# Second MLP layer of eight chunks as seven block products: attention and MLP on one Trainium2 core

## The chip, the cores and the metric

The kernel runs on one core of one Trainium2 chip. The metric is the device time of one execution in microseconds. A profiled execution gives a span, from the first to the last instruction; the runs without a profile give the time that counts.

## The reference

Four sequences of 768 tokens, 8 heads of 64. Attention looks at 4 sink tokens and a window of 128; then a layer norm with gain, a two-layer MLP (512 to 2048 to 512) and the residual:

```python
scores = scale * q @ k.T ; keep = (pos < 4) | (0 <= rel < 128)
a = softmax(where(keep, scores, -1e9)) ; x = concat_heads(a @ v)        # 3072 x 512
xn = (x - mean(x)) / sqrt(var(x) + 1e-6) * g_ln
out = x + max(xn @ w_ch1, 0.0) @ w_ch2
```

## The kernel before

The 3072 tokens are 24 tiles of 128; two tiles are a *chunk*, so there are 12 chunks, c = 0 to 11. Matmuls are in bf16 with fp32 sums in PSUM.

A small planner (`Plan`) is part of the kernel: each operation is given the engines that it may run on, a cost on each, a priority (a due time made from the numbers in `PAR`) and the buffers that it reads and writes. `P.run()` lists them by a model of the engines, picks the engine and buffer, and so fixes every engine's order when the program is built. On the chip each engine goes through its own list and waits for semaphores. Tiles that change hands are taken from rings; the ring `one` has four PSUM banks, `pair` has two slots of two banks.

What a chunk goes through:

- Loads. k, q and v of a chunk are loaded by POOL's queue (`nat`, L712; `vn`, L654). From chunk 4 on, SP turns k and q by DMA transposes into `kT` and `qT` (L586). The loads of a later chunk wait for the `rs` operation of an earlier tile (`gate`).
- Attention, from tile 6 on, in `block(t)`: PE does the value products of tile t - 1 (L962, L969 for the sinks, L978), then the scores of tile t (L989) and, for an even tile, the sink scores of the chunk (L997, into a bank of ring `one`). ACT takes the exponential (L1007, L1017), DVE multiplies with the band mask (L1012). For tile t - 1 DVE takes the reciprocal (L1030) and x (L1032).
- `normalise`: DVE takes the statistics of x (L890, L892) and subtracts the mean, giving `xc` (L894). POOL makes rstd = (var + 1e-6)^-0.5 in two instructions, `rs` (L899, L900). SP transposes xc into `xnt`.
- `mlp(c)`, first layer: eight pieces `ph`, u = 0 to 7, each 8 matmuls with 256 columns (both tiles of the chunk, L1055); ACT or DVE takes the relu into a bf16 tile of 512 (`h1`, L1065, L1067). xnt is not scaled by rstd: the relu and both layers pass a positive factor through.
- `mlp(c)`, second layer: for each tile 16 matmuls with 512 columns add up in one bank (L1083). DVE multiplies with rstd and adds x in one instruction (L1092); SP stores the tile (L1096).

On PE chunk c's second layer stands around the blocks of tiles 2c + 4 and 2c + 5: 24 matmuls between the two, 8 behind the second.

Of the kernel before, what the change touches and what calls it, by code (L numbers as in the profile page):

```python
# [7 lines left out]
FP32 = mybir.dt.float32  # L8
# [202 lines left out]
def fix(occ, extra=0.09):  # L211
# [22 lines left out]
PAR = dict(strict=400.0, win=0.4, tr=-8.0, sc=-5.0, sc1=-2.0, av=2.0, blk=-8.0, step=6.0, trx=9.0, by_dma=4, x_by_dma=2,  # L234
           w1p=(1.6, 2.6, 2.7, 2.8), pm=3, w2p=(4.5, 4.51, 4.52, 4.53), apart=2, vs0=(2.0, 13.0), by_tile=0, vp=(0.0, 0.1, 2.0, 2.1, 4.55, 4.56), ld1=0.05, t0=0.8, warm=7.9, pm0=-40.0, w1g=17.0, gtt=1.25)


def general(tc, nc, slots, pairs, ones, ident_f, ident, w1, w2, mhalf, g_s, g_r, q, k, v, out, scale):
# [14 lines left out]
    xs, os_, xn, xnt, h1 = slots["ot"][0:2], slots["ot"][2:4], slots["xc"][0], slots["xnt"][0], slots["h1"]  # L253
# [117 lines left out]
def kernel(  # L371
# [12 lines left out]
    nc = tc.nc  # L384
# [42 lines left out]
    ring("h1", 34, [128, 512], BF16)  # L427
# [138 lines left out]

    recs = []
# [9 lines left out]
    rs_op, trx_op = {}, {}  # L577

# [9 lines left out]
    def by_pairs(c, what, d):  # L588
# [13 lines left out]
        def tr(e):  # L602
            for nat, pt in zip(nats, pts):
                for hp in range(HP):
# [12 lines left out]
                 writes=[x for pt in pts for x in pt], mode="h" if whole else "q")  # L617
        for (nm, src, T, ld), pt in zip(what, pts):
# [43 lines left out]
    def chunk(c):  # L662
# [3 lines left out]
        if c < 2:  # L666
            kT_b[c], qT_b[c] = Buf(f"kT{c}", "kT"), Buf(f"qT{c}", "qT")
            if c == 0:
                nats = [Buf("kf", "natf"), Buf("qf", "natf")]
                for hh in range(2):  # L670
                    hs = slice(4 * hh, 4 * hh + 4)
                    for i, (x, T) in enumerate(((k, kT_b[c]), (q, qT_b[c]))):
# [6 lines left out]
                        P.op(f"cast{nm}{hh}", {"DVE": dve(512), "ACT": act(512)}, d + 0.01 * hh,  # L679
                             lambda e, nat=nat, src=src, hs=hs: (nc.scalar.copy if e == "ACT" else V.tensor_copy)(  # L680
                                 nat.t, src.t[:, hs].rearrange("p h i d -> p i h d")),
                             reads=[part], hold=[src], writes=[nat])
# [204 lines left out]
    def normalise(c, i, d, st, x, xc):  # L887
# [6 lines left out]
        P.op(f"xc{t}", {"DVE": fix(0.26)}, d + 0.14, lambda e: V.tensor_scalar(  # L894
            xc.t, x.t, st.t[:, 14:15], None, op0=ALU.subtract), reads=[x, st, mv], writes=[xc])
        rs = Buf(f"rs{t}")
        xst_b[t, "rs"] = rs
        rs_op[t] = P.op(f"rs{t}", {"POOL": (0.83, 0.88)}, d + 5, lambda e: (
            G.tensor_scalar(st.t[:, 17:18], st.t[:, 15:16], 1e-6, None, op0=ALU.add),  # L899
            G.tensor_tensor(st.t[:, 16:17], st.t[:, 17:18], mhalf, op=ALU.pow)),  # L900
            reads=[st, mv, Bc["mhalf"]], writes=[rs])
        pt = Buf(f"ptx{t}", "one")
# [21 lines left out]
    def block(t):  # L924
        c, i, b, r = t // 2, t % 2, t // RB, t % RB
        d = at(c, "blk") + PAR["step"] * i
        last = held.get(t - 1)
        reads, writes, hold = [], [], []
        if t < NT:
# [8 lines left out]
            pp_s = Buf(f"pss{c}", "one") if sinks else None  # L938
# [3 lines left out]
            writes += pps + ([pp_s] if sinks else [])  # L942
# [15 lines left out]
        def go(e):  # L958
# [33 lines left out]
            if sinks:  # L992
                for hp in range(HP):
                    for qh in range(2):
                        u = hp // 2
                        p0 = 64 * (qh ^ u) + 32 * (hp % 2)
                        nc.tensor.matmul(pp_s.t[p0:p0 + 32, 128 * u + 64 * (not r):128 * u + 128], lhsT=kts_b[b].t[:, hp, :],  # L997
# [5 lines left out]
        if t < NT:  # L1003
# [11 lines left out]
            if sinks:  # L1015
                lo = 0 if r else 64
                P.op(f"sx{c}", {"ACT": act(256 - 2 * lo)}, d + 0.3, lambda e: nc.scalar.activation(  # L1017
                    held["ps", c].t.rearrange("p (u c) -> p u c", u=2)[:, :, lo:128],
                    pp_s.t[:, 0:256].rearrange("p (u c) -> p u c", u=2)[:, :, lo:128], AF.Exp, scale=scale),
                     reads=[pp_s], writes=[held["ps", c]])  # L1020
# [16 lines left out]
    def mlp(c):  # L1037
        T = 16.0 * c + 8.0
        xnt = xnt_b[c]
        h1 = []  # L1040
        by_tile = c < PAR["by_tile"]
        for u in range(NH1 // 2):
            ph, hb = Buf(f"ph{c}_{u}", "one"), Buf(f"h{c}_{u}", "h1")

            def mm_t(e, u=u, ph=ph):
                for s in range(4):
                    for j in range(NDM):
                        nc.tensor.matmul(ph.t[:, 128 * s:128 * s + 128], lhsT=w1[u // 2][:, j, 128 * s:128 * s + 128],
                                         rhs=xnt.t[:, j, 128 * (u % 2):128 * (u % 2) + 128], start=j == 0, stop=j == NDM - 1)
# [9 lines left out]
            o = P.op(f"ph{c}_{u}", pe(0.944 if by_tile else 0.872), pr, mm_t if by_tile else mm, reads=[xnt_t[2 * c + u % 2] if by_tile else xnt, Bw1g[u // 2] if c >= PAR["x_by_dma"] else Bw1[u // 2][u % len(Bw1[u // 2])]],  # L1059
# [3 lines left out]
            def rl(e, ph=ph, hb=hb):  # L1063
                if e == "ACT":
                    nc.scalar.activation(hb.t, ph.t, AF.Relu)  # L1065
                else:
                    V.tensor_scalar_max(hb.t, ph.t, 0.0)  # L1067
            P.op(f"rl{c}_{u}", {"ACT": act(512), "DVE": dve(512)}, pr - 3, rl, reads=[ph], writes=[hb])
            h1.append(hb)
        T += 8  # L1070
# [144 lines left out]
```

## Time and profile before

| | us |
|---|---|
| runs: median of 3 (lowest to highest) | 215.67 (214.85 to 216.92) |
| profiled execution: its span | 213.8 |
| PE busy | 207.7 (97%) |
| DVE busy | 113.9 (53%) |
| ACT busy | 110.9 (52%) |
| POOL busy | 113.7 (53%) |

The profiled execution's own time is its span plus what lies around it; no time without the profiler is given for it, and the median of the runs is 1.87 us above its span. PE is TensorE's matmuls, PEld its weight loads, DVE VectorE, ACT ScalarE, POOL GpSimd, SP the queue of stores and transposes. L1083 is line 1083 of the kernel before. Lines of the profile have the form: line, engine, operation, written tile <- read tiles, shape, count | busy us in all, mean ns of one | idle time ahead of them and what ended it.

### The profile page before, as it was taken

The page shows a single profiled execution, that of the slowest core. Times are in us where ns is not written, and L with a number is a line of the kernel's source. Part 1 is how long each engine was busy: PE and PEld are TensorE (multiplying, and loading weights), DVE is VectorE, ACT ScalarE, POOL GpSimd, SP SyncE. Part 2 cuts the span into 40 slices and gives each one's busy share as a digit, 9 for nine tenths or more (in the row PEclk, how much of TensorE's full clock was granted, in tenths as well). Part 3 has the DMA queues.
Part 4 walks back from the last instruction along what each step waited for, and adds up shares of the span by engine and source line. Part 5 has one row for each costly group of instructions (what it writes and reads, how often), then busy time and mean ns, then how long its engine had stood idle before and what let it go on. Part 6 is the DMA issues. An engine that isn't in the chain of part 4 may idle for free.

```text
span 213.8 us, 6555 instructions
## 1 busy us (share of the span) xinstructions
PE 207.7 (97%) x2699; PEld 143.0 (67%) x2699; DVE 113.9 (53%) x316; ACT 110.9 (52%) x182; POOL 113.7 (53%) x169
## 2 busy tenths in 40 slices
PE   7799999999999999999999999999999999999994
PEld 2458965755865865865865865864865865865853
DVE  5598876896365356356355456356355345444021
ACT  3798797285652652562662562562562562530610
POOL 7969842489727980980970980971970401202000
PEclk9999999999999999999999999999999999999999
DMA  5999999999999998999899899899899902202103
GB/s 153 190 188 199 190 208 194 171 178 148 142 216 144 140 129 125 117 142 187 110 148 140 112 148 127 126 143 152 109 143 143 95 3 74 77 0 74 52 0 107
DMA packets 105642, 28.04 MB, mean 131 GB/s; under 512 B 94852, under 2 KB 102664, under 8 KB 105608
## 3 DMA queue, kind: packets, MB, share of 16 engines
q0 software_dynamic: 70960, 13.18, 83.6%
q1 hardware_dynamic: 33448, 13.71, 34.8%
q10 hardware_dynamic: 1200, 0.69, 1.1%
q8 instruction: 22, 0.36, 0.7%
q14 instruction: 12, 0.10, 0.2%
HBM read 27.43 MB, written 6.29 MB: 158 GB/s over the span
## 4 chain that ended last, share of the span: by engine, by line
PE 89%; DMA 5%; DVE 3%; ACT 1%; issue 1%; ACTq 0%; DVEq 0%
PE one L1083 40%; PE one L1055 37%; DMA qT<-nat 3%; PE pair L989 3%; DMA natf<-in_q_dram 3%; PE one L962 2%; PE one L969 2%; PE one L978 1%; PE one L997 1%; DVE st L890 1%; DVE x L882 1%; PE pair L614 1%; PE pair L739 1%; PE one L867 0%; PE pair L867 0%
## 5 line engine op out<-in xcount | busy, mean ns | idle before, releaser
L1083 PE MATMUL one<-w,h 128*128 128x512 bf16 (+2 forms) x400 | 87.4, 371 | 0.0
L1055 PE MATMUL one<-xnt,w 128*128 128x256 bf16 x768 | 86.8, 273 | 0.2 <-issue 0.2
L1055 PEld LDWEIGHTS <-w 128*128 128x128 bf16 x768 | 74.7, 98 | 11.5 <-issue 0.4
L1065 ACT ACTIVATE h<-one 128x512 bf16<-128x512 f32 x94 | 56.2, 598 | 45.7 <-PE one L1055 45.7
L1083 PEld LDWEIGHTS <-h 128*128 128x128 bf16 x400 | 37.1, 98 | 40.1 <-DMA w<-in_moe_w_ch_dram 0.2
L1007 ACT ACTIVATE pe<-pair 128x768 bf16<-128x768 f32 x36 | 27.2, 808 | 41.9 <-PE pair L989 41.9
L654 POOL DMA_DIRECT2D vn<-in_v_dram x59 | 38.8, 702 | 8.5 <-DMA w<-in_moe_w_ch_dram 6.8
L899 POOL TENSOR_SCALAR st<-st 128x1 f32<-128x1 f32 x24 | 9.0, 375 | 63.8 <-DVE st L892 63.3
L1030 DVE RECIPROCAL rec<-one 128x4 f32<-128x4 f32 x36 | 6.4, 178 | 62.7 <-PE one L978 51.3
L1092 DVE SCALAR_TENSOR_TENSOR ot<-one,st,x 128x512 f32<-128x512 f32 (+2 forms) x25 | 18.2, 728 | 20.0 <-PE one L1083 13.7
L900 POOL TENSOR_TENSOR st<-st,mhalf 128x1 f32<-128x1 f32 x24 | 16.4, 682 | 2.0
L890 DVE BATCH_NORM_STATS2 st<-x 128x6 f32<-128x512 bf16 x24 | 16.7, 695 | 0.8
L1032 DVE TENSOR_TENSOR x<-one,rec 128x256 bf16<-128x256 f32 x36 | 15.3, 425 | 1.2
L712 POOL DMA_DIRECT2D nat<-in_k_dram x16 | 14.9, 935 | 1.8 <-DMA natp<-in_q_dram 1.4
L712 POOL DMA_DIRECT2D nat<-in_q_dram x16 | 14.4, 914 | 0.0
L1012 DVE TENSOR_TENSOR pe<-pe,band 128x768 bf16<-128x768 bf16 x24 | 12.2, 552 | 0.0
L894 DVE TENSOR_SCALAR xc<-x,st 128x512 bf16<-128x512 bf16 x24 | 8.9, 373 | 0.9
L989 PE MATMUL pair<-qT,kT 64*64 64x128 bf16 (+1 forms) x528 | 9.2, 204 | 0.0
L962 PEld LDWEIGHTS <-pe 128*128 128x128 bf16 (+1 forms) x144 | 6.2, 97 | 2.9 <-issue 1.3
L787 ACT ACTIVATE pe<-pair 128x1024 bf16<-128x1024 f32 (+1 forms) x8 | 7.1, 916 | 0.8 <-PE pair L739 0.4
L989 PEld LDWEIGHTS <-kT 64*64 64x64 bf16 x528 | 7.2, 108 | 0.4 <-ACT w L1119 0.4
L962 PE MATMUL one<-vn,pe 128*128 128x65 bf16 (+1 forms) x144 | 7.0, 193 | 0.0
(112 smaller groups left out, 152.3 us busy)
## 6 DMA issues: line engine op xcount, KB each, us to landing
out_dram<-ot SPq DMA_DIRECT2D x23, 256.0 KB
w<-in_moe_w_ch_dram POOLq DMA_DIRECT2D x6, 512.0 KB, 13.5
nat<-in_k_dram POOLq DMA_DIRECT2D x16, 128.0 KB, 5.0
nat<-in_q_dram POOLq DMA_DIRECT2D x16, 128.0 KB, 5.3
vn<-in_v_dram POOLq DMA_DIRECT2D x44, 32.0 KB, 5.3
w<-in_moe_w_ch_dram POOLq DMA_DIRECT2D x4, 256.0 KB, 10.9
vn<-in_v_dram POOLq DMA_DIRECT2D x15, 64.0 KB, 5.1
natp<-in_k_dram POOLq DMA_DIRECT2D x3, 256.0 KB, 6.7
```

Of the source, the lines that this page charges most:

```text
L654: P.op(f"vld{t}_{i}", {"POOL": (0.8, 0.85)}, prio + 0.001 * i, lambda e, p0=p0, n=n, hs=hs, src=src: G.dma_start(m.t[p0:p0 + n, hs, 0:64], ...
L712: lambda e, nat=nat, ap=ap: G.dma_start(nat.t, ap), writes=[nat], dma=SW, after=gate(c))
L890: P.op(f"bn{t}", {"DVE": fix(0.60)}, d + 0.12, lambda e: V.bn_stats(st.t[:, 8:14], x.t), reads=[x], writes=[st, mv])
L900: G.tensor_tensor(st.t[:, 16:17], st.t[:, 17:18], mhalf, op=ALU.pow)),
L962: nc.tensor.matmul(po[h // 4].t[:, 65 * (h % 4):65 * (h % 4) + 65], lhsT=pe_[rs, col:col + 128], rhs=vn_b[t - 1].t[rs, h, :], start=h % 4 ...
L989: nc.tensor.matmul(pps[u].t[64 * g:64 * g + 64, h2, col + c0:col + c0 + n], lhsT=kt.t[rs, hp, k0:k0 + 64], rhs=qT.t[rs, hp, q0:q0 + n], st ...
L1007: nc.scalar.activation(pes[j].t.rearrange("p a b -> p (a b)")[:, 0:768].rearrange("p (a b) -> p a b", a=2), pps[j].t[:, :, 0:384], AF.Exp, ...
L1032: P.op(f"x{t - 1}{u}", {"DVE": dve(256)}, d + 0.051 + 0.002 * u, lambda e, u=u, rc=rc, pv=pv: V.tensor_tensor(x.t[:, 256 * u:256 * u + 256 ...
L1055: nc.tensor.matmul(ph.t[:, 256 * s:256 * s + 256], lhsT=w1[ht // 4][:, j, 128 * (ht % 4):128 * (ht % 4 + 1)], rhs=xnt.t[:, j, :], start=j ...
L1065: nc.scalar.activation(hb.t, ph.t, AF.Relu)
L1083: nc.tensor.matmul(pc.t[:, 0:wd], lhsT=(h1[2 * s + i].t[:, 128 * ii:128 * ii + 128] if by_tile else h1[ht // 2].t[:, 256 * (ht % 2) + 128 ...
L1092: V.scalar_tensor_tensor(ot.t[:, sl], in0=pc.t[:, 0:wd], scalar=st.t[:, 16:17], in1=x.t[:, sl], op0=ALU.mult, op1=ALU.add),
```

## The change

For chunks 3 to 10 the second layer is done as a 2x2 block product: the two tiles of the chunk (i = 0, 1) times the two halves of the inner dimension, and the two halves of the output columns. Seven products of half size take the place of eight, in the form with sums shared between them. The two factors of a product are a half of h1 or a sum of halves, and a half of w2 or a difference of halves:

- `w2t`: four differences of w2's quarters, made once, in the tiles of the rings `natf` and `natp`, which are not used any more by then (8 operations, given to DVE).
- Sums of h1, per chunk: s3, s1, s2, s4, two operations each (L1090 of the kernel after), in a new ring `sb`, which also takes over the slots of `natc`.
- Products P1 to P7 (L1113): each 8 matmuls with 256 columns. P1, P6, P5 and P3 go through one bank, b0; between them the running sum is copied out (k1, k6, k5) while the bank goes on adding. P2 is in b1, P7 and then P4 in b2.
- Output quarters: o11 = b1 + k1, o22 = b2 + k5, o21 = b2 + k6 (L1123), o12 a copy (L1119). Then x is added, 512 wide (L1150, DVE or POOL; the order gives it to DVE).

Since sums over tokens of different tiles must have one scale, rstd is put on xc for these chunks: `rs` comes ahead of xc, and xc (L914) takes mean and rstd. Sink scores go to the unused columns of the second scores bank. h1 has 16 tiles of 1024 instead of 34 of 512. Blocks stand earlier by up to 6 steps (`lead`), the second block of a chunk later (`step`).

```diff
-PAR = dict(..., step=6.0, ...)
+PAR = dict(..., step=8.0, ..., seven=3, lead=(0, 0, 0, 2, 4, 6), w2t=-4.0, at7=(0.5, 1.5, 2.5, 3.5, 4.5, 6.5, 7.5))
...
-    ring("h1", 34, [128, 512], BF16)
+    ring("h1", 16, [128, 1024], BF16)
+    ring("sb", 6, [128, 4, 128], BF16)
+    P.rings["sb"] += [Slot(..., o.name, o.units) for o in P.rings["natc"]]
+    ring("tx", 4, [128, 256], FP32)
...
+    def by_seven(c):
+        return PAR["seven"] <= c < NC - 1
...
-        P.op(f"xc{t}", {"DVE": fix(0.26)}, d + 0.14, lambda e: V.tensor_scalar(
-            xc.t, x.t, st.t[:, 14:15], None, op0=ALU.subtract), reads=[x, st, mv], writes=[xc])
...
+        if not by_seven(c):
+            P.op(f"xc{t}", ...)
-        rs_op[t] = P.op(f"rs{t}", {"POOL": (0.83, 0.88)}, d + 5, lambda e: (
+        rs_op[t] = P.op(f"rs{t}", {"POOL": (0.83, 0.88)}, d + (0.135 if by_seven(c) else 5), lambda e: (
...
+        if by_seven(c):
+            P.op(f"xc{t}", {"DVE": fix(0.26)}, d + 0.14, lambda e: V.tensor_scalar(
+                xc.t, x.t, st.t[:, 14:15], st.t[:, 16:17], op0=ALU.subtract, op1=ALU.mult),
+                reads=[x, st, mv, rs], writes=[xc])
...
-        d = at(c, "blk") + PAR["step"] * i
+        d = at(c, "blk") + PAR["step"] * i - PAR["lead"][min(c, len(PAR["lead"]) - 1)]
...
-                        nc.tensor.matmul(pp_s.t[p0:p0 + 32, 128 * u + 64 * (not r):128 * u + 128], lhsT=kts_b[b].t[:, hp, :],
+                        nc.tensor.matmul(pps[1].t[p0:p0 + 32, u, 384 + 64 * (not r):512], lhsT=kts_b[b].t[:, hp, :],
...
+    def second_by_seven(c, T, h1):
+        def half(m, i):
+            return h1[m].t.rearrange("p (a n) -> p a n", a=4)[:, :, 128 * i:128 * i + 128]
+        def add(n, m, d, in0, in1, op, reads):
+            b = sums[n, m] = Buf(f"s{n}_{c}{m}", "sb")
+            P.op(f"s{n}_{c}{m}", {"DVE": dve(512, 0.64)}, d, lambda e: V.tensor_tensor(b.t, in0(), in1(), op=op),
+                 reads=reads, writes=[b])
+        for m in range(2):
+            add(3, m, T - 3.6 + 2 * m, lambda m=m: half(m, 0), lambda m=m: half(m, 1), ALU.subtract, [h1[m]])
+        for m in range(2):
+            add(1, m, T - 1.2 + m, lambda m=m: half(m, 1), lambda m=m: half(m + 2, 1), ALU.add, [h1[m], h1[m + 2]])
+            add(2, m, T - 1.1 + m, lambda m=m: sums[1, m].t, lambda m=m: half(m, 0), ALU.subtract, [h1[m], sums[1, m]])
+            add(4, m, T - 0.5 + m, lambda m=m: half(m + 2, 0), lambda m=m: sums[2, m].t, ALU.subtract, [h1[m + 2], sums[2, m]])
...
+        def product(p, bank, d, new=False, after=()):
+            def mm(e):
+                for m in range(2):
+                    for a in range(4):
+                        nc.tensor.matmul(bank.t[:, 0:256], lhsT=left[p](m)[:, a, :], rhs=right[p](m)[:, a, :],
+                                         start=new and m + a == 0, stop=m + a == 4, skip_group_check=True)
+            P.op(f"P{p}_{c}", pe(0.875), d, mm, reads=[*needs[p], *w_of[p]], after=after, ...)
...
+        product(1, b0, T + at[0], True)
+        o1 = keep("k1", T - 8, b0, [k1], lambda: k1.t)
+        product(7, b2, T + at[1], True)
+        product(6, b0, T + at[2], after=[o1])
+        o6 = keep("k6", T - 8, b0, [k6], lambda: k6.t)
+        product(2, b1, T + at[3], True)
+        plus("o11", T + at[3], b1, [ot[0], oo[0][0]], lambda: ot[0].t[:, lo], k1)
+        product(5, b0, T + at[4], after=[o6])
+        o5 = keep("k5", T - 8, b0, [k5], lambda: k5.t)
+        o22 = plus("o22", T + at[4], b2, [ot[1], oo[1][0]], lambda: ot[1].t[:, hi], k5)
+        product(3, b0, T + at[5], after=[o5])
+        keep("o12", T + at[5], b0, [ot[0], oo[0][1]], lambda: ot[0].t[:, hi])
+        product(4, b2, T + at[6], after=[o22])
+        plus("o21", T + at[6], b2, [ot[1], oo[1][1]], lambda: ot[1].t[:, lo], k6)
+        # per tile: o (ot + x) and the store
```

The order on PE in a period of the chunks 3 to 9 is now: even block, pieces 2 to 7 of the first layer, P1, P7, odd block, P6, P2, P5, piece 0 of the next chunk, P3, piece 1, P4, and the next even block.

How the rows stand, at three places. First DVE, around an odd and the following even block of a chunk in the middle. Before, a block's statistics are followed by xc, two mask products, and the one instruction that makes an output tile:

```order
162 L890 BN_STATS st_190<-x_126 128x6
163 L892 BN_AGGR st_190<-st_190 128x2
164 L894 TENSOR_SCALAR xc_136<-x_126,st_190 128x512
165 L1012 TENSOR_TENSOR pe_108<-pe_108,band_200 128x768
166 L1012 TENSOR_TENSOR pe_109<-pe_109,band_201 128x768
167 L1092 TENSOR_SCALAR ot_179<-one_63,st_187,x_123 128x512
```

In the change (h, sb and natc hold h1 and its sums, tx the kept copies):

```order
243 L1119 COPY tx_167<-one_65 128x256
244 L1046 TENSOR_TENSOR x_130<-one_63,rec 128x256
245 L900 BN_STATS st_186<-x_130 128x6
246 L902 BN_AGGR st_186<-st_186 128x2
247 L1026 TENSOR_TENSOR pe_104<-pe_104,band_192 128x768
248 L1026 TENSOR_TENSOR pe_105<-pe_105,band_193 128x768
249 L914 TENSOR_SCALAR xc_134<-x_130,st_186 128x512
250 L1123 TENSOR_TENSOR ot_170<-one_66,tx_165 128x256
251 L1123 TENSOR_TENSOR ot_171<-one_64,tx_166 128x256
252 L1150 TENSOR_TENSOR ot_170<-ot_170,x_126 128x512
253 L1123 TENSOR_TENSOR ot_171<-one_64,tx_167 128x256
254 L1150 TENSOR_TENSOR ot_171<-ot_171,x_127 128x512
```

xc has moved behind the mask products and now needs POOL's rstd; behind it stand o11, o22, the additions of x and o21. After an even block the eight sums (L1090) stand in the place of these.

Second POOL, between the two blocks of a chunk. Before, all v loads come ahead of the odd block's rstd (L899, L900):

```order
107 L654 DMA vn_89<-in_v_dram 64x4x64 x4
108 L654 DMA vn_90<-in_v_dram 128x4x64
109 L654 DMA vn_90<-in_v_dram 64x4x64 x2
110 L899 TENSOR_SCALAR st_195<-st_195 128x1
111 L900 TENSOR_TENSOR st_195<-st_195,mhalf 128x1
112 L899 TENSOR_SCALAR st_180<-st_180 128x1
```

and in the change:

```order
107 L664 DMA vn_89<-in_v_dram 64x4x64 x4
108 L910 TENSOR_SCALAR st_187<-st_187 128x1
109 L911 TENSOR_TENSOR st_187<-st_187,mhalf 128x1
110 L664 DMA vn_90<-in_v_dram 128x4x64
111 L664 DMA vn_90<-in_v_dram 64x4x64 x2
112 L910 TENSOR_SCALAR st_172<-st_172 128x1
```

The rstd of the odd block has moved ahead of the last v loads; the four loads of k and q and four of v stay between the even block's rstd and it.

Third PE, where the sink scores of block 8 end (kts are the sinks, w_3 is the last quarter of w1, h a relu). Before, the second layer of chunk 2 follows:

```order
1713 L997 LDWEIGHTS kts_115
1714 L997 MATMUL one_64<-qT_97,kts_115 32x128
1715 L1083 LDWEIGHTS h_158
1716 L1083 MATMUL one_65<-w_0_223,h_158 128x512
1719 L1083 LDWEIGHTS h_159
```

and in the change the last piece of chunk 2's first layer:

```order
1697 L1011 LDWEIGHTS kts_115
1698 L1011 MATMUL pair_61<-qT_97,kts_115 32x128
1699 L1062 LDWEIGHTS w_3_214
1700 L1062 MATMUL one_65<-xnt_140,w_3_214 128x256
```

The block has moved ahead of that piece, so PE reaches its sink scores one piece (8 matmuls) sooner.

100 lines of the change are left out of this document (74 added, 26 removed).

## The prediction

> **What bounds the kernel now.** I read the page first, then the chain that ended last, then the busy time by stretches, then the groups by form. The page's first part and its clock row:
>
> ```profile
> PE 207.7 (97%) x2699; PEld 143.0 (67%) x2699; DVE 113.9 (53%) x316; ACT 110.9 (52%) x182; POOL 113.7 (53%) x169
> PEclk9999999999999999999999999999999999999999
> ```
>
> TensorE is busy for 207.7 of 213.8 us, at a granted clock that no slice shows reduced; the other engines stand near half. A busy PE proves little by itself, so the chain has to say whether anything else ends a step. One steady period, from one first layer to the next (start, length, piece):
>
> ```profile
> 117.52 6.99 PE one L1055 x64
> 124.51 0.24 PE one L962 x8
> ...
> 125.69 5.29 PE one L1083 x24
> 130.98 0.24 PE one L962 x8
> ...
> 131.94 1.83 PE one L1083 x8
> 133.77 0.33 PE one L1055 x3
> ```
>
> The chain runs from PE to PE without a gap: first layer 6.99, even attention block 1.18 (124.51 to 125.69), 24 matmuls of the second layer 5.29, odd block 0.96, the last 8 in 1.83: a period of 16.25 us. The stretches say the same, and how much room the others have:
>
> ```profile
> 117.50:133.80 16.30, 16.30 (x227) 11.44 (x225) 8.59 (x24) 8.08 (x13) 10.24 (x15) 1.00 1.35 129
> 133.80:149.70 15.90, 15.90 (x198) 10.93 (x197) 8.00 (x21) 7.97 (x13) 9.76 (x14) 1.00 1.31 140
> ```
>
> The columns after the length are PE, PEld, DVE, ACT, POOL, clock and DMA. PE fills its stretch at clock 1.00; DVE has 8.0 to 8.6 of 16. So PE work removed is time removed, as long as nothing else grows to the period. DVE is where this change puts its work, so DVE decides.
>
> **What it removes on PE.** A chunk's second layer was 32 matmuls of 512 columns; it becomes seven products of 8 matmuls with 256 columns, 56 in all.
>
> ```profile
> L1055 PE MATMUL one<-xnt,w 128*128 128x256 bf16 x768 | 86.8, 273 | 0.2 <-issue 0.2
> L1083 PE MATMUL one<-w,h 128*128 128x512 bf16 x368 | 83.9, 380 | 0.0
> L1055 PEld LDWEIGHTS <-w 128*128 128x128 bf16 x768 | 74.7, 98 | 11.5 <-issue 0.4
> ```
>
> The means here overlap, since matmuls are pipelined; the spacing comes from the chain. 24 in 5.29 us is 220 ns each at 512 columns; 64 in 6.99 us is 109 ns each at 256. A weight load of 98 ns still fits under a 109 ns matmul, as the first layer does it all the time. Before: 32 x 0.220 = 7.05 us. After: 56 x 0.109 = 6.12 us. That is 0.93 us a chunk and, for the eight chunks 3 to 10, **7.4 us**. A product (8 matmuls) takes 0.874 us.
>
> One rule speaks against this. The Trainium skill (TensorE: Matmul & The Clock Gate, Back-to-back issue gap) gives a stream of weight-load and matmul pairs a sustained spacing of about 81 ns at 128 columns and 131 ns at 512, far from proportional to width. By it the 32 wide matmuls would cost an estimated 4.2 us and 56 narrow ones over 4.5 (81 ns each at the least), so the product would lose. The spacings of this trace, 220 and 109 ns, do not agree with it: they follow the width, and I take the trace.
>
> **What it adds on DVE.** Rows for the price (by form; busy, then mean ns):
>
> ```profile
> L1012 DVE TENSOR_TENSOR pe<-pe,band 128x768 bf16<-128x768 bf16 x24 | 12.2, 552 | 0.0
> L790 DVE TENSOR_TENSOR pe<-pe,mask 128x1024 bf16<-128x1024 bf16 x2 | 1.3, 686 | 0.0
> L882 DVE TENSOR_TENSOR x<-pair,rec 128x512 bf16<-128x512 f32 x2 | 1.4, 691 | 0.1
> L1032 DVE TENSOR_TENSOR x<-one,rec 128x256 bf16<-128x256 f32 x36 | 15.3, 425 | 1.2
> L1092 DVE SCALAR_TENSOR_TENSOR ot<-one,st,x 128x512 f32<-128x512 f32 x23 | 17.2, 749 | 18.1 <-PE one L1083 13.0 <-POOL st L900 5.0
> L1067 DVE TENSOR_SCALAR h<-one 128x512 bf16<-128x512 f32 x2 | 1.4, 688 | 1.2 <-ACT qT L659 1.2
> L890 DVE BATCH_NORM_STATS2 st<-x 128x6 f32<-128x512 bf16 x24 | 16.7, 695 | 0.8
> L892 DVE BATCH_NORM_AGGREGATE st<-st 128x2 f32<-128x6 f32 x24 | 4.4, 182 | 0.8
> L894 DVE TENSOR_SCALAR xc<-x,st 128x512 bf16<-128x512 bf16 x24 | 8.9, 373 | 0.9
> L1030 DVE RECIPROCAL rec<-one 128x4 f32<-128x4 f32 x36 | 6.4, 178 | 62.7 <-PE one L978 51.3
> ```
>
> The attention side of a period (4 reciprocals, 4 x, 2 statistics, 2 aggregates, 4 mask products, 2 xc) is 0.71 + 1.70 + 1.39 + 0.36 + 2.21 + 0.75 = 7.12 us and stays. Two L1092 (1.50) go. Added per chunk: eight bf16 sums of 512. No row has that shape; between 768 elements (552) and 1024 (686) the slope is 0.52 ns an element, which gives 0.42 us; the other bound is 512 elements at full length, 0.69 (L882). I take 0.42, since the sums are bf16 in SBUF like L1012: 3.4 us. Then three sums out of PSUM with 256 elements (0.425 each, 1.3), two additions of x with 512 (0.75 at most, 1.5), one copy of k6 (0.425) and one relu that the order now gives to DVE (0.69). Sum: 7.12 + 3.4 + 1.3 + 1.5 + 0.4 + 0.7 = **14.4 us of DVE** in a PE period of 16.25 - 0.93 = 15.3. It fits, with 94% by durations that partly overlap (x to the next instruction is 0.35 us below, not 0.425). ACT gains up to three copies of 256 (at most 0.425 each) on 8.0 and stays far below.
>
> DVE fitting in the sum is not enough; its order is fixed, and two places are tight. One attention block on DVE and POOL in the trace (start, length):
>
> ```profile
> 125.44 0.42 DVE L1032 TENSOR_TENSOR x<-one,rec 128x256 bf16<-128x256 f32 x1
> 125.79 0.17 DVE L1030 RECIPROCAL rec<-one 128x4 f32<-128x4 f32 x1
> 125.99 0.42 DVE L1032 TENSOR_TENSOR x<-one,rec 128x256 bf16<-128x256 f32 x1
> 126.45 0.69 DVE L890 BATCH_NORM_STATS2 st<-x 128x6 f32<-128x512 bf16 x1
> 127.18 0.18 DVE L892 BATCH_NORM_AGGREGATE st<-st 128x2 f32<-128x6 f32 x1
> 118.76 1.86 POOL L712 DMA_DIRECT2D nat<-in_k_dram  x2
> 120.61 1.77 POOL L712 DMA_DIRECT2D nat<-in_q_dram  x2
> 122.34 4.48 POOL L654 DMA_DIRECT2D vn<-in_v_dram  x7
> 127.46 0.38 POOL L899 TENSOR_SCALAR st<-st 128x1 f32<-128x1 f32 x1 [0.63 <-DVE st L892]
> 127.92 0.73 POOL L900 TENSOR_TENSOR st<-st,mhalf 128x1 f32<-128x1 f32 x1
> ```
>
> First place: **product 4 waits for o22**, since both use bank b2, and o22 stands behind the odd block's xc, which now waits for rstd from POOL. From the end of product 6: k6 copy 0.35, second x 0.46, statistics 0.73 (aggregate starts at 1.6), rstd done 1.47 after the aggregate's start (127.18 to 128.65), so at 3.05, xc 0.27, o11 0.35, o22 0.425: 4.1 us. PE meanwhile has products 2, 5, 3 and two pieces of the next first layer, 5 x 0.874 = 4.37. It passes with 0.2 to 0.3 us, from which the signals still go. Bounds: nothing, up to 0.4 a period where rstd is slow; I take 0.1, so 0.8 us in eight periods (0 to 3.2). Behind the waiting xc stand the eight sums, the k copies and the reciprocals; PE waits for all of them.
>
> Second place: **POOL must be free** when the odd aggregate is ready. The order puts 8 loads between the two rstd: 4 of k and q (118.76 to 122.34, 3.6 us) and 4 of v (4.48/7 each, 2.6 us). With the 1.47 of the even rstd that is 7.6 us. From even to odd aggregate there are about 7.7: the even one starts 2.7 us after its block's end (the relu waits until 0.9, then 0.6, x 0.46, statistics 0.73), the odd one 1.6 after product 6, which ends 6.99 + 0.96 + 0.87 = 8.8 us after that block (six pieces of first layer, two products, block, product). It fits by 0.1 us; if late, it enters the first place one for one and is in its bounds.
>
> **What it moves.** The blocks move forward, and what they read does not. Block 2c = 8 now stands before the last piece of chunk 2's first layer. Its sink matmuls wait for qT already now (the wait row of the weight loads, then the chain):
>
> ```profile
> PEld L997 <- DMA qT<-nat: 0.2, 1, 0.2
> 54.57 6.12 DMA qT<-nat
> 60.77 0.29 PE one L997 x8
> ```
>
> The SP and POOL rows before that transfer stand in the same order in the change, so qT lands at 60.7 as before, PE comes 0.87 us sooner and stands **0.9 us** (0 if the transfer comes as much sooner). Later blocks come about 6 us sooner against the first layer; the order gives their transposes an earlier place past the output stores, and I count no more.
>
> Once, before chunk 3, eight differences of w2 (1024 elements, 0.686: 5.5 us) go to DVE.
>
> ```profile
> 36.00:58.00 22.00, 22.00 (x295) 14.63 (x294) 16.18 (x36) 12.80 (x22) 16.51 (x25) 1.00 1.80 161
> ```
>
> DVE had 5.8 us free there, so they are hidden by DVE's idle time; some sit ahead of mask products, so 0.3 us (0 to 1.0). The sink scores only change their bank, and the stores on SP stay one a tile: nothing is counted for them.
>
> **The sum.** On the profiled execution: 213.8 - 7.4 + 0.9 + 0.8 + 0.3 = 208.4 us of span. The runs shown have a median of 215.67, 1.87 above that span; with it **210.3 us**. The bounds of the terms: 215.67 - 7.4 = 208.3 and 215.67 - 7.4 + 0.9 + 3.2 + 1.0 = 213.4.
>
> **The rivals.**
>
> *rstd arrives late and takes the gain.* In the change the mask products start right behind the aggregate, at the moment when POOL starts rstd. The two POOL lines (min/median/max):
>
> ```profile
> L899 POOL TENSOR_SCALAR st<-st x24: 220/378/753, 14.8 to 192.1; 128x1 f32<-128x1 f32 x24
> L900 POOL TENSOR_TENSOR st<-st,mhalf x24: 566/729/737, 15.1 to 192.7; 128x1 f32<-128x1 f32 x24
> ```
>
> They are already up to 0.53 and 0.17 us longer at some places than at others, so something on the chip holds them. Held for the whole of both mask products (1.1 us) instead of the few tenths in which the sum has them, xc and o22 would come some 0.8 us late in each of eight periods: 210.3 - 0.8 + 6.4 = 215.9 us, no change. For it: both tight places hang on POOL. Against it: in the trace the pow beside a mask product takes 0.73, not 1.1. The Trainium skill (SBUF — State Buffer, on the port pair that VectorE and GpSimd share) says a VectorE instruction with two SBUF inputs and a GpSimd one that reads SBUF exclude each other for a whole instruction; the 0.73 us agrees only in part.
>
> *The sums run at full length and DVE becomes the bound (the slow side).* Each source is four strips of 128 with gaps. At L882's 0.69 us a sum, DVE has 14.4 + 8 x 0.27 = 16.6 us, and twice 0.35 of waiting for rstd (1.47 less the masks' 1.1): 17.3 against the old 16.25. Eight periods: +8.4, with 0.9 and 0.3: 225 us. It decides from 0.56 us a sum ((16.25 - 14.4 - 0.7) / 8 above 0.42). Against it: strips are contiguous, as in L1012. The Trainium skill (VectorE: DVE Perf Modes, What auto-detection actually checks) asks only for 16 bits and step 1, which these have; no row here shows strips.
>
> *Price by instruction, not by column.* If a narrow matmul took half the way between 109 and 220 ns, 56 would take 9.2 us, +2.2 a chunk, 215.7 + 17 = 233 us. The first layer's 109 ns over 64 in a row leaves it almost nothing. This is the direction of the Trainium skill's rule on the issue gap, weighed above.
>
> **How the numbers follow.** Forecast 0.68; late rstd 0.16; full-length sums 0.13; price by instruction 0.01; slower by something unnamed 0.02. About 1% can be told from no change here, so below 213.5 is faster and above 217.8 slower: faster 0.68, same 0.16, slower 0.16. The forecast's own range is 208.3 to 213.4. The range for 8 in 10 takes in the late rstd at 215.9: 208.3 to 216.0, which leaves out the slow cases, 0.16.
>
> **What would show it.** Right: products at 109 ns a matmul; period near 15.4 us; PE busy near 201 of 208; sums near 0.42 us and DVE at 85 to 95% of chunks 3 to 10; one wait of about 1.1 us for qT at block 8; waits of PE for DVE under 0.2 us a period. Wrong: sums above 0.56 us; xc lines waiting for POOL by more than half a us, with a PE gap ahead of product 4; POOL idle nowhere between loads and rstd; later blocks waiting for qT or kT.

## The result, and the profile after

The change measured 212.91 us as the median of 4 runs (212.21 to 216.34) beside 215.81 for the kernel before (214.85 to 216.92): ratio 0.986, interval 0.982 to 0.990. In a second set it measured 214.88 over 12 runs (212.40 to 216.00) beside 215.63: ratio 0.992 (0.989 to 0.995). By these ratios it is faster by 0.8 to 1.4%, 1.7 to 2.9 us, where 5.4 were forecast (the medians over all runs differ by 0.75 us in the second set and 2.9 in the first); both medians lie in the range (208.3 to 216.0), the first inside the forecast's own range (208.3 to 213.4), the second outside. The ratios leave out runs over 1.5% above a kernel's fastest; the change scatters so widely that this cuts 1 run in 4 and 3 in 12 of its own, so lowest and highest are given with every median. The profiled execution took 212.65 us, with a span of 211.1.

The page of the change, its engines and its clock:

```profile
PE 202.0 (96%) x2891; PEld 161.2 (76%) x2891; DVE 156.8 (74%) x426; ACT 116.0 (55%) x200; POOL 114.3 (54%) x169
PEclk9999999999999999999999999999999999999999
```

PE's busy time fell by 5.7 us, but the span by 2.7 only: idle time of PE has come in. The part of the chain that ended last shows it, from one attention block to the first piece of the next chunk (L1062, the first layer), and then a period without a stall (L1113 are the products):

```profile
91.52 0.19 DVE st L902
91.79 0.44 POOL st L910
92.31 0.74 POOL st L911
93.07 0.41 DVE xc L914
93.49 0.44 DVE natc L1090 x2
93.93 6.12 DMA xnt<-xc
100.10 1.05 PE one L1062 x8
...
104.94 5.35 PE one L1062 x48
110.29 1.75 PE one L1113 x16
...
113.00 2.73 PE one L1113 x24
115.72 0.87 PE one L1062 x8
...
120.44 5.35 PE one L1062 x48
...
156.24 6.57 DMA xnt<-xc
162.85 1.05 PE one L1062 x8
```

The chain before ran from PE to PE at this place. Now it leaves PE: aggregate, rstd on POOL, xc, the DMA transpose of xc into xnt, and only then the piece. The waits of PE between 55 and 190 us say how much (total, times, longest):

```profile
PE one L1062 <- DMA xnt<-xc: 1.1, 2, 0.8
PE one L1062 <- DVE pe L1026: 1.0, 2, 0.6
PE pair L1011 <- DMA qT<-nat: 0.7, 1, 0.7
```

The second row names a mask product that ended long before; at those places (84.03 and 146.98) the landing records of the trace put xnt at 83.90 and 146.93, so it is the transfer too. In the same view of the kernel before, no row stands at all. Then the new sums and the reason why xc is late (groups by form, DVE, 55 to 200 us):

```profile
L1090 DVE TENSOR_TENSOR sb<-h,h 128x512 bf16<-128x512 bf16 x10 | 4.2, 420 | 0.0
L914 DVE TENSOR_SCALAR xc<-x,st 128x512 bf16<-128x512 bf16 x16 | 6.6, 413 | 7.3 <-POOL st L911 7.0
```

A sum takes 420 ns. xc waits for rstd, 7.0 us over the 14 tiles where it does.

### The profile page after: what moved, and what is told of

Its sections match the earlier page's. It is cut to its first block, busy times and chain, and to the rows that moved or that the text cites. A ratio compares the mean times of both kernels' runs of the same rounds, so it can differ in the third digit from the quotient of the medians.

```text
span 211.1 us, 7043 instructions
## 1 busy us (share of the span) xinstructions
PE 202.0 (96%) x2891; PEld 161.2 (76%) x2891; DVE 156.8 (74%) x426; ACT 116.0 (55%) x200; POOL 114.3 (54%) x169
## 4 chain that ended last, share of the span: by engine, by line
PE 74%; DMA 12%; DVE 9%; ACT 2%; POOL 1%; issue 1%; ACTq 0%; DVEq 0%
PE one L1062 33%; PE one L1113 17%; PE one L1167 13%; DMA xnt<-xc 6%; DMA qT<-nat 3%; DMA natf<-in_q_dram 3%; DVE st L900 2%; PE pair L1003 2%; PE one L976 2%; PE one L983 1%; DVE x L1046 1%; PE one L992 1%; PE pair L1011 1%; ACT qT L669 1%; POOL st L911 1%
## 5 line engine op out<-in xcount | busy, mean ns | idle before, releaser
L1062 PE MATMUL one<-xnt,w 128*128 128x256 bf16 x768 | 89.8, 273 | 2.1 <-DMA xnt<-xc 1.1
L1062 PEld LDWEIGHTS <-w 128*128 128x128 bf16 x768 | 73.5, 98 | 13.6 <-DMA xnt<-xc 2.3
L1073 ACT ACTIVATE h<-one 128x512 bf16<-128x512 f32 x87 | 52.0, 598 | 40.1 <-PE one L1062 39.0
L1167 PE MATMUL one<-w,h 128*128 128x512 bf16 (+2 forms) x144 | 29.5, 356 | 0.1
L1167 PEld LDWEIGHTS <-h 128*128 128x128 bf16 x144 | 13.4, 98 | 12.3 <-DMA w<-in_moe_w_ch_dram 0.4
L1113 PEld LDWEIGHTS <-h 128*128 128x128 bf16 x192 | 18.8, 98 | 2.5 <-issue 0.2
L900 DVE BATCH_NORM_STATS2 st<-x 128x6 f32<-128x512 bf16 x24 | 16.6, 693 | 0.7
L1113 PE MATMUL one<-w,h 128*128 128x256 bf16 x128 | 16.6, 273 | 0.1
L1113 PEld LDWEIGHTS <-sb 128*128 128x128 bf16 x156 | 15.0, 98 | 1.9
L1123 DVE TENSOR_TENSOR ot<-one,tx 128x256 f32<-128x256 f32 x24 | 9.5, 420 | 7.5 <-PE one L1113 4.9
L1175 DVE SCALAR_TENSOR_TENSOR ot<-one,st,x 128x512 f32<-128x512 f32 (+2 forms) x9 | 6.2, 691 | 11.6 <-PE one L1167 10.3
L1119 ACT COPY tx<-one 128x256 f32<-128x256 f32 x17 | 6.3, 372 | 14.7 <-PE one L1113 14.7
L722 POOL DMA_DIRECT2D nat<-in_q_dram x16 | 14.4, 912 | 0.0
L1150 DVE TENSOR_TENSOR ot<-ot,x 128x512 f32<-128x512 f32 x16 | 11.1, 692 | 3.1 <-ACT ot L1119 2.7
L914 DVE TENSOR_SCALAR xc<-x,st 128x512 bf16<-128x512 bf16 x16 | 6.6, 413 | 7.3 <-POOL st L911 7.0
```

What stands on the lines that cost most here:

```text
L722: lambda e, nat=nat, ap=ap: G.dma_start(nat.t, ap), writes=[nat], dma=SW, after=gate(c))
L900: P.op(f"bn{t}", {"DVE": fix(0.60)}, d + 0.12, lambda e: V.bn_stats(st.t[:, 8:14], x.t), reads=[x], writes=[st, mv])
L1062: nc.tensor.matmul(ph.t[:, 256 * s:256 * s + 256], lhsT=w1[ht // 4][:, j, 128 * (ht % 4):128 * (ht % 4 + 1)], rhs=xnt.t[:, j, :], start=j ...
L1073: nc.scalar.activation(dst, ph.t, AF.Relu)
L1113: nc.tensor.matmul(bank.t[:, 0:256], lhsT=left[p](m)[:, a, :], rhs=right[p](m)[:, a, :], start=new and m + a == 0, stop=m + a == 4, skip_g ...
L1150: V if e == "DVE" else G).tensor_tensor(ot[i].t, ot[i].t, x.t, op=ALU.add), reads=[ot[i], *oo[i], x], writes=[done])
```

## The experiments

**Theory A:** the missing gain is (1) a PE saving that I took too large, and (2) PE waiting for xnt at a chunk's first piece, because xnt is issued later (rstd ahead of xc) and lands late behind output stores and transposes of k on SP's queue. **Rivals:** B, the earlier blocks cost it by themselves; C, DVE's load or order; D, the landing does not depend on when xnt is issued; E, the traffic of the loads, not the place in the queue, makes the landing slow.

**1. The products alone taken out.** All chunks have the plain second layer, and the differences of w2 go with the products; tokens and blocks are as in the change, so the last addition there adds x without rstd. The main hunk:

```diff
-        if by_seven(c):
-            second_by_seven(c, T + 8, h1)
-        else:
-            second(c, T + 8, h1)
+        second(c, T + 8, h1)
```

Expected: 

> Leaves out the seven products: chunks 3 to 10 have the plain second layer of eight pieces, but their tokens carry rstd and their blocks stand as early as in the change. Theory A (the stalls come from the seven products pulling the next chunk's first piece ahead of the landing of its second tile): the first piece of a chunk now stands behind eight plain pieces, xnt has 2.6 us more after the odd block, and no piece waits for it; period 16.2 us as before, only block 8 still loses 0.6 us at qT: ratio 1.000 to 1.004. Rival B (the earlier blocks or rstd ahead of the tokens cost the 2.2 us by themselves): the same stalls of about 2 us and the 0.6 us on top of the time before: ratio 1.010 to 1.015.

Measured 216.32 us (215.21 to 217.70), ratio 1.004 (1.001 to 1.006). Its waits of PE between 55 and 190 us:

```profile
PE pair L1011 <- DMA qT<-nat: 1.2, 1, 1.2
PE pair L1003 <- DMA qT<-nat: 0.7, 1, 0.7
```

No piece waits for xnt, though the transposes land hardly sooner after their issue than in the change (by the landing records of chunks 3 to 9, 4.8 to 6.6 us against 5.2 to 6.6); they are there 1.1 to 3.5 us ahead of the piece. B falls: blocks and rstd without the products cost 0.4%, in the profile all at qT. It is the products, which end a chunk sooner and let the next chunk's first piece in between them, that use the slack up.

**2. rstd put on at the end.** Tokens centred only, as before; the last addition becomes output times rstd plus x. (Each output row is one token's, so the algebra allows it; only the rounding of the bf16 sums speaks for a scale on the tokens.)

```diff
-        if by_seven(c):
-            P.op(f"xc{t}", ... V.tensor_scalar(xc.t, x.t, st.t[:, 14:15], st.t[:, 16:17], op0=ALU.subtract, op1=ALU.mult), ...
+        # xc as before, ahead of rstd
...
-                V if e == "DVE" else G).tensor_tensor(ot[i].t, ot[i].t, x.t, op=ALU.add)
+                ot[i].t, in0=ot[i].t, scalar=st.t[:, 16:17], in1=x.t, op0=ALU.mult, op1=ALU.add)
```

Expected: 

> Seven products, but the tokens are only centred as before, and rstd is put on in the last addition (output times rstd plus x, one operation on VectorE). Theory A: the tokens and with them the transposes leave about 0.5 us sooner per tile, the five stalls shrink by 0.3 to 0.5 us each: 1.5 us less than the change, ratio 0.977 to 0.981. Rival C (VectorE's load or order makes the stalls): VectorE gets the additions that GpSimd shared, so the stalls stay or grow: ratio 0.986 or above. Rival D (the transposes of k ahead in the queue set the landing, whenever xnt is issued): landing unchanged, ratio 0.986.

Measured 212.66 us (210.35 to 215.80), ratio 0.983 (0.980 to 0.986), profiled span 210.1. The interval touches A's range and overlaps that of the change, and over all twelve runs the median is 0.987 of the kernel before's; the time alone shows no gain over the change. The profile shows less waiting: xc waits for rstd no more, and two stalls for xnt remain (0.3 and 0.8 us, with 1.0 for qT). The earlier issue is partly lost again: by the landing records the transposes that feed a first piece land 0.4 to 1.5 us sooner, with latencies still from 5.0 to 7.8 us. So D is right in part: something other than the issue of xnt sets its landing. C is not supported, but hardly tested either: DVE is busy 0.6 us longer in all, since its order had all these additions before.

**3. xnt ahead of the transposes of k.**

```diff
-                        reads=[nat], writes=[T], dma=HW_X, after=[trx_op[2 * c - 3]] if c > PAR["by_dma"] and nm == "q" else [])
+                        reads=[nat], writes=[T], dma=HW_X, after=[trx_op[2 * c - 3]] if c > PAR["by_dma"] else [])
```

Expected: 

> The change with one difference: on SP's queue the transposes of k of a chunk above 4 also stand behind the last xnt of the chunk before, as those of q already do; so xnt has no transposes of k ahead of it. Theory A with the queue as the cause of the late landing: xnt lands within 4 to 5 us of its issue instead of 5.8 to 6.6, the stalls of PE for xnt fall below 0.5 us in total, ratio 0.975 to 0.979, if k comes in time. Rival E (traffic of the loads, not the place in the queue, makes the landing slow): still 5.5 us or more and stalls of 2 us: ratio 0.984 to 0.988. Rival F (k comes too late): the waits move to the score matmuls of the even blocks, ratio 0.986 or above.

Measured 224.19 us (222.50 to 226.67), ratio 1.037 (1.033 to 1.041). Its waits of PE:

```profile
PE pair L1011 <- DMA qT<-nat: 10.5, 4, 4.0
PE one L1113 <- DVE ot L1123: 0.4, 1, 0.4
```

No row for xnt is left: with no transposes of k ahead, it lands 2.5 to 4.4 us after its issue (landing records, chunks 3 to 9). And qT, now behind k which is behind xnt, takes 10.5 us in four waits: rival F, with a ratio far above its 0.986. Part of the time is a reduced clock behind these waits (last section). The queue's order decides what PE waits for. The transposes are all needed, so they cannot be put behind each other at no cost; the next edit moves something that nobody waits for.

**4. Lighter loads of v.** From tile 13 on a load reads one of its heads only, so the attention there works on old values of v. SP's queue stays as it is.

```diff
+            if t >= 13:
+                hs, src = slice(hs.start, hs.start + 1), src[:, 0:1, :]
```

Expected: 

> The change, but the loads of v of tiles 13 on read only one of their heads: as many transfers, a fraction of the bytes (the rest of v is old data). Rival E (the traffic of the loads makes the landing slow): xnt lands in under 5 us, the stalls fall below 0.8 us in total, ratio 0.976 to 0.980. Theory A with the queue as the cause: still 5.5 us or more behind the transposes of k, stalls of 2 us, ratio 0.984 to 0.988.

Measured 211.50 us (209.98 to 213.15), ratio 0.981 (0.977 to 0.985). Waits for xnt sum to 1.3 us in the profile instead of 2.1. By the landing records the transposes ahead of a first piece (chunks 5 to 9) took 6.6 us once, then 3.8, 3.4, 3.0 and 5.3, where the change has 6.1, 6.1, 5.8, 6.2 and 6.6. The change's second profile (experiment 5) has 8.0, 4.5, 4.7, 6.1 and 4.6, so a part of this is its own scatter, and the two intervals of the ratio overlap. E seems to hold in part: traffic counts beside the place in the queue, by how much is not shown.

**5. The change again, and the stores moved.** The change was run again as a base (second set above).

Expected: 

> The change itself once more, beside the three that follow, for its own scatter: ratio 0.982 to 0.990 by what was measured before. If the landing of the transposes sets the stalls, its runs scatter more than those of the kernel before (1.7 us from lowest to highest of 23), since no wait of PE for a transfer stands in that one.

It scattered over 3.6 us, the kernel before over 2.2 beside it, so the wider scatter came as expected; the ratio, 0.992, missed the expected interval (0.982 to 0.990). In its profile PE waits 4.0 us for xnt and 1.4 for qT, twice the first profile's. In the next run only the stores move on SP:

```diff
+                after=[trq_op["q", c + 4]] if c + 4 < NC else [trx_op[2 * c + 5]] if 2 * c + 5 < NT else [])
```

Expected: 

> The change, with the two output stores of a chunk issued on SP behind the transposes of q of the chunk four further on, instead of between and ahead of the transposes of k; the order on all other engines is the same. Theory A with the queue as the cause: the transposes of k and then xnt land 1 to 2 us sooner, the stalls of PE for xnt (2.1 us) fall below 0.5, ratio 0.975 to 0.980. Rival E (traffic of the loads makes the landing slow, the place in the queue does not): landing unchanged, ratio 0.984 to 0.990. Rival G (the stores, now late, hold the output buffers or the next transposes): new waits ahead of the products or the score matmuls, ratio 0.988 or above.

Measured 211.86 us (211.04 to 212.35), ratio 0.982 (0.979 to 0.985): 1% faster than the change beside it, and the scatter is down to 1.3 us. SP's queue in the change (start and length of the issue), then with late stores:

```profile
87.87 0.50 SPq L1151 DMA_DIRECT2D out_dram<-ot  x1
89.35 1.32 SPq L595 DMA_TRANSPOSE kT<-nat  x1
91.18 0.34 SPq L1151 DMA_DIRECT2D out_dram<-ot  x1
91.64 2.19 SPq L595 DMA_TRANSPOSE kT<-nat  x1
93.93 1.20 SPq L595 DMA_TRANSPOSE xnt<-xc  x1
```

```profile
89.42 3.44 SPq L595 DMA_TRANSPOSE kT<-nat  x2
94.20 1.20 SPq L595 DMA_TRANSPOSE xnt<-xc  x1
95.52 2.50 SPq L595 DMA_TRANSPOSE qT<-nat  x2
98.11 1.96 SPq L1151 DMA_DIRECT2D out_dram<-ot  x2
```

xnt is issued at the same time, but lands after 3.8 us (98.03) instead of 6.1 (100.05); over chunks 5 to 9 it is 3.7 to 4.5 us, where the change's two profiles have 4.5 to 8.0. The waits of PE:

```profile
PE one L1062 <- DMA xnt<-xc: 1.3, 1, 1.3
PE pair L1011 <- DMA qT<-nat: 0.7, 1, 0.7
PE one L1062 <- DVE ot L1123: 0.4, 1, 0.4
```

From chunk 5's first piece on PE waits for xnt nowhere. Left are 1.3 us at chunk 4's, ahead of which no moved store stands; that is more than A's 0.5, and the ratio ends just short of A's 0.980. The last row is new (102.14): a piece waits for a bank that DVE frees (L1123) right behind an xc that had waited 0.47 us for rstd; DVE stood for no output buffer there. This settles the place in the queue as a cause, against E alone and G.

**6. The same stores in the kernel before.** If A is right they buy nothing there.

Expected: 

> The kernel before the change, with one difference: the output stores of chunks 3 to 10 issued on SP behind the transposes of q of the chunk four further on. Theory A: PE waits for no transfer in that kernel (0.8 to 2.3 us of slack at each chunk's first piece), so the sooner landing buys nothing: ratio 0.998 to 1.003. Rival H (late stores are a gain of their own, whatever the second layer): 0.990 to 0.995. Rival G (late stores hold output buffers): above 1.005.

Measured 216.02 us (215.39 to 217.81), ratio 1.003 (1.001 to 1.005): no gain, so rival H is out. The profile shows one new wait for xnt (2.3 us at 152.00), so it sits between A and a small loss.

**7. Blocks 8 and 9 back in their old place**, with the late stores, and then with rstd at the end as well.

```diff
-  lead=(0, 0, 0, 2, 4, 6)
+  lead=(0, 0, 0, 2, 0, 6)
```

Expected: 

> As the run with the late stores, and blocks 8 and 9 stand where they stood before the change (block 8 behind the last piece of chunk 2's first layer). Theory A: the wait of 0.7 us for qT at block 8 goes too, and block 10 has its transposes in time: ratio 0.972 to 0.978. Rival: block 9 is late for chunk 4's tokens and the 0.7 us comes back at chunk 4's first piece: ratio as that of the run with the late stores.

Expected: 

> Late stores, blocks 8 and 9 back, and rstd put on in the last addition instead of on the tokens. Theory A: xnt has another 0.5 us and more of slack, nothing of PE's waits for transfers is left between 55 and 190 us: span near 208, ratio 0.968 to 0.976. Rival C (VectorE, which now has all last additions, becomes late with sums or bank copies): waits of PE for VectorE of over 1 us in total, ratio 0.978 or above.

Measured 212.70 (212.08 to 214.44), ratio 0.987 (0.984 to 0.991), and 210.86 (210.43 to 212.44), ratio 0.979 (0.976 to 0.983). The wait for qT at block 8 is gone in both, and comes back larger at chunk 4's first piece. In the first run PE waits 3.3 us there: xc ended at 78.75, but its transpose was issued at 81.37 only, behind two of k, the first of which had waited 3.0 us for its load. In the second, 1.5 us: the issue is no later than in the change (77.81 against 78.17), but the landing took 6.1 us and PE came sooner. That row names DVE (L1119), as C would have it; but xnt landed at 83.95, 0.13 us ahead of the piece, as at this piece in the other runs that wait, so it is the transfer. The rival named for the first run was right on the place, though not on the size (0.987 beside 0.982); the second run missed A's figure by this one wait.

**8. All blocks back** (lead 0, step 6), seven products.

Expected: 

> The seven products with the blocks back where they stood before the change (lead 0, step 6). From the even block to the next chunk's first piece PE then has seven products and the odd block, about 8.8 us, where the change has 12.3; from that block's end to the landing of xnt the change took 11.7 us in the trace (88.4 to 100.05). Theory A (the path block, tokens, transposes, first piece is what PE waits for): a stall of 2 to 3 us in each of eight chunks, ratio 1.06 to 1.11. Rival B (the moved blocks are what costs): no stalls and no wait for qT at block 8, ratio 0.965 to 0.985.

Measured 219.21 us (218.75 to 220.19), ratio 1.018 (1.014 to 1.022). Both figures missed. xnt costs only 1.2 us of PE's waits here; the rest is this row:

```profile
PE one L976 <- DVE ot L1123: 6.5, 7, 0.9
```

and one such place, PE and DVE:

```profile
115.13 0.41 DVE L914 TENSOR_SCALAR xc<-x,st 128x512 bf16<-128x512 bf16 x1 [0.47 <-POOL st L911]
115.46 0.42 DVE L1090 TENSOR_TENSOR sb<-h,sb 128x512 bf16<-128x512 bf16 x1
115.80 0.75 DVE L1123 TENSOR_TENSOR ot<-one,tx 128x256 f32<-128x256 f32 x2
116.27 0.37 PE L976 MATMUL one<-vn,pe 128*128 128x65 bf16 x7 [0.94 <-DVE ot L1123]
```

The attention block needs a PSUM bank that o11 (L1123) frees, and o11 stands on DVE behind a sum and the xc that waits for POOL. This is the wait behind rstd that the prediction priced at product 4, at another reader: with the blocks close behind the products PE stands 0.9 us a chunk, of which rstd is 0.47 here and the order on DVE the rest. With the blocks moved PE does not wait there. The moved blocks belong to the change, not to its cost.

**9. Late stores and rstd at the end, blocks as in the change**, and a variant with other leads (2 in place of 4 for blocks 8 and 9, 8 in place of 6 for blocks 10 and 11).

Expected: 

> Late stores and rstd in the last addition, blocks placed as in the change. Theory A: waits for qT at block 8 (0.7 to 1.0 us) and at chunk 4's first piece (0.5 to 1.0 us) remain, none later: span 208.5 to 209.5, ratio 0.974 to 0.980, scatter under 2 us. Rival C (VectorE late with all the last additions): waits for VectorE of over 1 us, ratio above 0.982.

Expected: 

> As the run before it, with block 9 two pieces later and block 10 as early as the change has it. Theory A: chunk 4's first piece waits under 0.7 us, qT at block 8 about 0.7: ratio 0.972 to 0.979. Rival: block 9 later makes block 10's masks and with them chunk 4's tokens later, and the wait at chunk 4's first piece is 1 us or more: ratio 0.979 to 0.984.

The first measured 210.30 us (210.02 to 213.86), ratio 0.975 (0.972 to 0.978), span 208.5; the second 210.91 (210.00 to 213.31), ratio 0.978 (0.975 to 0.982). The first beats both kernels: 2.5% faster than before, and 0.7% beyond late stores alone (0.982 in another set, the intervals apart), so rstd off the path of xnt is worth about that much here. Its scatter was expected under 2 us, and one of the six runs lies 3.5 above the others. The profile of the variant, of its slowest run, has the wait that its rival named: 2.1 us at chunk 4's first piece. The first version's waits of PE for a transfer between 55 and 190 us, all of them:

```profile
PE pair L1007 <- DMA qT<-nat: 0.5, 1, 0.5
```

Two of its periods by stretches (columns as in the prediction), and the first piece that opens each in the chain:

```profile
100.20:115.70 15.50, 15.50 (x251) 13.81 (x249) 13.09 (x35) 8.65 (x16) 10.08 (x16) 1.00 1.58 138
115.70:131.20 15.50, 15.50 (x251) 13.79 (x250) 13.89 (x37) 8.65 (x16) 10.82 (x17) 1.00 1.57 140
```

```profile
99.00 0.87 PE one L1058 x8
...
114.46 0.87 PE one L1058 x8
...
129.91 0.87 PE one L1058 x8
```

PE fills the stretches. DVE has 13.1 to 13.9 us in a period of 15.5 and no wait of PE between 55 and 200 us that is put down to it is over 0.14 us, so C is out.

## Why the prediction was right in its sign and too large

- **The PE term was mis-sized.** The step "24 in 5.29 us is 220 ns each at 512 columns" took in a start of about 0.11 us that PE needs behind an attention block, whatever the width: the 48 narrow matmuls behind a block show the same (5.35 us, against 48 x 0.1092 = 5.24), and so do the 24 products in 2.73. Without it the wide spacing is 5.18 / 24 = 216 ns, as the matmuls also stand from start to start in the trace, and the saving 32 x 0.216 - 56 x 0.1092 = 0.79 us a chunk, not 0.93. The unstalled periods agree: 104.94 to 120.44 is 15.50 in the change, 99.00 to 114.46 is 15.46 in the first version of experiment 9, against 16.25. Eight chunks: 6.3 us instead of 7.4. The same section of the Trainium skill that I weighed (TensorE: Matmul & The Clock Gate, Back-to-back issue gap) also gives columns / 2.4 + 2.5 ns for an isolated matmul: an estimate of 215.8 and 109.2 ns. The trace agrees with these two, and not with the sustained 131 ns that stands beside them.
- **The step "the order gives their transposes an earlier place past the output stores, and I count no more" failed.** I followed k and q there, but not xnt. Three things eat its slack, which was 0.6 to 2.3 us (chunks 3 to 9, from the landing to the first piece). xc is later: in the change it starts 1.55 us behind its aggregate (91.52 to 93.07), before 0.22:

```profile
95.04 0.18 DVE L892 BATCH_NORM_AGGREGATE st<-st 128x2 f32<-128x6 f32 x1
95.26 0.35 DVE L894 TENSOR_SCALAR xc<-x,st 128x512 bf16<-128x512 bf16 x1
95.64 1.19 SPq L586 DMA_TRANSPOSE xnt<-xc  x1
```

  The transfer lands later (100.49 for this one, 4.8 us; 6.1 in the change, behind two stores and two transposes of k). And the first piece stands two products sooner. From chunk 3's first piece to the end of chunk 11's first layer the timelines have 134.8 us before and 131.6 in the change: 3.1 gained where 6.3 were to be had, and the wait rows name 2.1 of the 3.2 lost as xnt. The other 1.1 has no row; a part of it is the overlap that a stalled stream loses, an estimate of up to 0.16 us at each of the five first pieces that waited (a matmul's record is 273 ns long, and in a stream the records stand 109 apart). The 210.30 us version of experiment 9, without stores ahead and without rstd ahead, takes 128.8 over the same stretch: 6.0 gained.
- **Product 4 behind rstd** (0.8 us) did not come: PE stands ahead of no product 4, though o22 ends only 0.05 to 1.0 us ahead of it. The pass was about as narrow as forecast. The wait can show at another reader: 0.4 us once in experiment 5, 0.9 a chunk in experiment 8.
- **Block 8 at qT**: 0.9 forecast, 0.7 in the profile, 0.4 to 1.4 in the others that keep the block there. Right.
- **The differences of w2**: 0.3 forecast. No row of PE waits for them; whether a part of chunk 3's period is theirs was not tried.
- **The sums**: 0.42 us forecast, 0.420 measured, so the slow rival (full length) is out; DVE has 12.0 to 13.9 us in the three periods of the change from 84.03 to 131.28, below the 14.4 that were added up. The price by instruction is out too: the 16 matmuls of two products take 1.75 us, 109 ns each.
- **rstd late** was given 0.16, with its place at o22. rstd was late, 0.47 us at 13 of 16 xc rather than 0.8 at each, and what it delayed was the transpose. The rival had one of the causes, and the wrong victim.
- **Added up** for the profiled span: 208.4 forecast, + 1.1 (PE term), - 1.1 (product 4 and w2), - 0.5 (chunk 3 starts 0.4 behind, at 69.39 against 68.97, not 0.9), + 3.2 (lost behind it) = 211.1, beside 211.1; the 3.2 is a remainder, not a sum of rows. The errors on PE and on DVE cancel; the size was missed by what the transfer took. That the version of experiment 9 lands on the forecast's 210.3 is that cancelling too, and so luck. The listed times lie 1.5 to 1.6 us above their spans, not 1.87.

## What to carry to other kernels

When a change shortens the bound engine's part, list every transfer that feeds it with its slack before, and subtract from that slack both the time the consumer comes sooner and each wait put ahead of the producer; the order alone does not give it, the issue time, what is ahead in the queue and the landing do. Put what nobody waits for, such as output stores, behind what someone waits for on the same queue. Take a spacing from the difference of two runs of different length, not from one run that begins behind a switch.

## What the runs showed of the hardware

- Waits for late transfers went with scattered times. The kernel before, with no such wait, stayed within 2.2 us; the change ranged over 3.6 and 4.1, with late stores over 1.3 (six runs). That the one makes the other is not shown. In experiment 9, five of the first version's six runs lie within 0.3 us; the sixth, 213.86, has a mean granted clock of 0.992, and what follows may be why. Four runs of the kernel before have 0.990 or 0.991, and no trace of these is kept.
- A stall of PE was at times followed by a lower clock, and so cost twice. In the variant of experiment 9 PE stood 2.1 us at 83.1 to 85.25 (each line: stretch, length, PE, PEld, DVE, ACT, POOL, granted clock, DMA, GB/s):

```profile
82.00:84.00 2.00, 1.14 (x11) 0.78 (x8) 1.96 (x6) 0.37 (x1) 1.34 (x3) 1.00 1.59 147
84.00:86.00 2.00, 0.75 (x6) 0.67 (x7) 1.05 (x5) 0.00 (x0) 2.00 (x3) 0.94 0.85 127
86.00:88.00 2.00, 2.00 (x12) 1.43 (x10) 0.00 (x0) 0.60 (x1) 2.00 (x3) 0.50 1.82 160
88.00:90.00 2.00, 2.00 (x15) 1.56 (x14) 1.02 (x2) 0.37 (x1) 2.00 (x4) 0.70 2.10 153
90.00:92.00 2.00, 2.00 (x63) 1.76 (x61) 1.64 (x5) 1.16 (x2) 0.73 (x2) 1.00 2.91 125
```

  The clock records have half rate from 85.78 to 89.19, 3.41 us, which would cost 1.7: from this first piece to the next chunk's are 16.76 us, beside 15.10 in the first version. The same followed the stall of 3.3 us in experiment 7, and in experiment 3 those of 4.0, 3.4 and 2.6. The stall of 2.3 us in the change's second profile left the clock at 1.00, so the length alone does not decide. The records suggest what does: in all twelve traces that have them, the clock changes only at whole multiples of 3.413 us behind the first record. With the traces cut on that grid from the first record on, each of nine stretches at full rate in which PE stood 1.88 us or more was followed by half rate, and none in which it stood 1.53 or less; the stall of 2.3 us falls on two stretches, 1.3 and 1.0. The Trainium skill (TensorE: Matmul & The Clock Gate, What's actually happening) has the half rate follow an idle window of about 3.4 us that runs free of the kernel; the half rate and its duration agree, but here a stall of 2.1 us within such a stretch was enough.
- DMA transposes of one size landed between 2.4 and 8 us after their issue, by what stood ahead of them on the queue (experiment 5) and perhaps by what the loads moved meanwhile (experiment 4).
